# A two-layer transformer kernel on one core: dense products as single float32 matmuls, weights kept as loaded, activations turned by TensorE

## The chip, the core and the metric

The kernel runs on one NeuronCore of a Trainium2 chip. The core has five engines with queues of their own: TensorE (PE in the profile; its weight loads are listed apart as PEld), VectorE (DVE), ScalarE (ACT), GpSimd (POOL) and SyncE (SP, which here issues most DMAs). The metric is the device time of one execution in microseconds (us). Matmul operands lie in SBUF (128 partitions), results in PSUM banks of 512 float32 values per partition.

## The reference

Two identical layers over 2048 rows of 640 values, each a sliding-window attention block and a feed-forward block, in float32:

```
def _A_ref(x, wqkv, wo):                       # H = 32 heads of Dh = 20, window W = 256
    qkv = (x @ wqkv).reshape(B, S, 3, H, Dh)
    scores = einsum("bhqd,bhkd->bhqk", q, k) * Dh ** -0.5
    scores = where(0 <= q_pos - k_pos < W, scores, -1e9)
    o = einsum("bhqk,bhkd->bhqd", softmax(scores), v)
    return o.reshape(B, S, D) @ wo

def _B_ref(x, w1, b1, w2, b2):                 # F = 1536
    h = x @ w1 + b1
    return relu(h) ** 2 @ w2 + b2

for layer in range(2):                         # the same weights in both
    x = x + _A_ref(layernorm(x), wqkv, wo)
    x = x + _B_ref(layernorm(x), w1, b1, w2, b2)
```

## The kernel before

**Tiling.** The 2048 rows are cut into 8 groups of T = 256 rows; with two layers that makes 16 units (`NU`), worked on one after the other. A unit has five dense stages and eight quads of attention. A quad is four heads.

**Dense stages.** `stage_qk` forms q and k turned (weights stationary, 256 columns of rows move), `stage_v` forms v (rows stationary, 320 columns move), `stage_o` multiplies the attention's output by `wo`, `stage_f` does both feed-forward products. All go through `mm3` (L335). Every operand is held as two float16 halves, `hi` and the remainder `low`, and a product is three matmuls of halves: hi x hi, hi x low, low x hi. Scales (`YS`, `WS`, `OS`) keep the halves in float16's range.

**How halves are made.** Weights: loaded as float32 into memory that is used later (`w1raw`, `w2raw`, `krow`, `vts`), then `convert` (L270) writes hi on ScalarE and low on VectorE. Normalized rows: for most units `cross` (L444) casts hi on ScalarE, subtracts low on VectorE, and turns each half by a crossbar transpose that SP's queue issues (`dma_start_transpose`); `ln_cross` and `ln_early` use it ahead of `stage_qk`, `y_cross` ahead of `stage_f`. Units 0 and 1, and three turns of `stage_y`, use `split_t` (L383) instead: TensorE transposes 3 and 2 blocks of 128 columns into a PSUM tile, ScalarE copies hi out, VectorE subtracts. The attention's output is split in `load_o` (L1023, L1026), the feed-forward's hidden values in `stage_f` (L1123, L1126).

**Attention.** For each quad `max_quad` puts scores into the PSUM banks `bb6` and VectorE takes row maxima (L719, L722); `exp_quad` puts the shifted scores into the same banks and ScalarE takes exponentials (L827), which POOL (L856) and VectorE (L865) mask; `pv_quad` multiplies them by v on TensorE in float32 (L933). `banks()` waits until the readers of the last scores are done. Maxima run three quads ahead (`LEAD`) and come back as rows through a crossbar transpose and a DMA (`max_cross`).

**Order.** All five engines run the order in which the program is recorded, and the recorder plans it with costs of its own. `post` queues a job for VectorE, ScalarE or POOL with a cost in ns, `step(ns)` moves TensorE's planned clock `now`, `Want` holds back a piece until its operands or one of two PSUM tiles (`mm`) should be free. `together` lays a unit's dense stages between its quads in proportion to their planned costs (`QKC`, `VC`, `OC`, `FCST`, `LNC`), and takes more dense work where a quad would wait. `mm3` books 109 ns for a matmul of 256 columns and 136 for 320:

```
for a, b in ((0, 0), (0, 1), (1, 0)):
    nc.tensor.matmul(acc, lhs(a, c), rhs(b, c), start=(k == 0), stop=(k == 3 * nk - 1))
```

`spin` (L350) runs float32 matmuls of the 128x128 identity at the start, 14 and then 7.

Of the kernel before, what the change touches and what calls it, by code (L numbers as in the profile page):

```python
# [16 lines left out]
P = 128  # L17
# [17 lines left out]
YS = 2.0 ** 10  # L35
WS = 2.0 ** 8
QS = 2.0 ** 3
OS = 2.0 ** 6
# [7 lines left out]
def kernel(ctx: ExitStack, tc: tile.TileContext, x, wqkv, wo, w1, b1, w2, b2, out):  # L46
# [49 lines left out]
    def set_sums(i):  # L96
        nc.vector.memset(vts[i][0][:, :, DH:DH + 1], 1.0 / OS)
        nc.vector.memset(vts[i][1][:, H * (DH + 1):], 0.0)
# [158 lines left out]
    wq_s = sb.tile([P, 2, KC, 3 * D], F16, name="wq_s")  # L257
    wo_s = sb.tile([P, 2, KC, D], F16, name="wo_s")
    w1_s = sb.tile([P, 2, KC, F], F16, name="w1_s")
    w2_s = sb.tile([P, 2, FC, D], F16, name="w2_s")  # L260
# [4 lines left out]
    w1raw = w1_s.rearrange("p a k n -> p (a k n)").bitcast(F32)  # L265
    w2raw = w2_s.rearrange("p a k n -> p (a k n)").bitcast(F32)
    hraw = sb.tile([P, 2 * FC * T // 2], F32, name="stg", tag="hh", bufs=1)
    gate, gate0, gate2 = [Job("S", 0.0, None, [], 0.0, 0) for i in range(3)]

    def convert(st, hi, low, n, load, *deps, prio=2):  # L270

        a = post("A", 20 + 0.9 * n, lambda: nc.scalar.activation(hi, st, AF.Copy, scale=WS), load, *deps, prio=prio)
        return post("D", 30 + 1.04 * n, lambda: nc.vector.scalar_tensor_tensor(low, st, WS, hi, op0=ALU.mult,
                                                                               op1=ALU.subtract), a, prio=prio)
# [3 lines left out]
    def load_wq():  # L278
        at = 0
        for lo, n in [(j * D + c, min(2 * P, D - c)) for c in (0, 2 * P, 4 * P) for j in range(2)] + [  # L280
                (2 * D + c, min(2 * P, D - c)) for c in (0, 2 * P, 4 * P)]:
            raw, o = (w1raw, at) if at + KC * n <= FC * D else (krow[2], at - FC * D)
            at += KC * n
            st = raw[:, o:o + KC * n].rearrange("p (c n) -> p c n", c=KC)
            load = dma(lambda st=st, lo=lo, n=n:
                       nc.sync.dma_start(st, wqkv[:, lo:lo + n].rearrange("(c p) n -> p c n", p=P)),
                       P * KC * n * 4, prio=0, land=WLAND)
            for z in range(0, n, P):
                c = slice(lo + z, lo + z + P)
                wqj[(lo + z) // P] = convert(st[:, :, z:z + P], wq_s[:, 0, :, c], wq_s[:, 1, :, c], KC * P, load,  # L290
                                             prio=1)
# [3 lines left out]
    def load_wo():  # L295

        v = wo.rearrange("(p c) n -> p c n", c=KC)
        raw = w2raw[:, (FC - KC) * D:].rearrange("p (c n) -> p c n", n=D)
        loads = []
        for c0, n in ((0, 2), (2, 3)):  # L300
            loads.append(bulk(lambda c0=c0, n=n: nc.scalar.dma_start(raw[:, c0:c0 + n], v[:, c0:c0 + n]), P * n * D * 4, gate0))
        for c in range(KC):
            woj[c] = convert(raw[:, c], wo_s[:, 0, c], wo_s[:, 1, c], D, loads[-1], *loads[:-1])
        rowset[1] = [post("D", 460, lambda k=k: set_row(1, k), prio=2) for k in range(4)]

    def load_w1():
        first = list(wqj.values())
        for f0 in (0, 6, 2, 8, 4, 10):
            st = w2raw[:, f0 * D:(f0 + 2) * D].rearrange("p (c n) -> p c n", c=KC)
            load = bulk(lambda st=st, f0=f0: nc.scalar.dma_start(  # L310
                st, w1[:, f0 * P:(f0 + 2) * P].rearrange("(c p) n -> p c n", p=P)), P * KC * 2 * P * 4, gate,
                *(woj.values() if (f0 + 2) * D > (FC - KC) * D else ()))
            for f in (f0, f0 + 1):
                c = slice(f * P, (f + 1) * P)
                w1j[f] = convert(st[:, :, (f - f0) * P:(f - f0 + 1) * P], w1_s[:, 0, :, c], w1_s[:, 1, :, c], KC * P,
                                 load, *first)

    sums = []

    def load_w2():  # L320
        used_by = {}
        for c, place in enumerate((3, 4, 0, 1, 2, 0, 1, 2, 0, 1, 2, 0)):
            first = [w1j[f] for f in (c // 4 * 2, c // 4 * 2 + 1, 6 + c // 4 * 2, 7 + c // 4 * 2)]
            st = vts[1 + place][1][:, :D] if place > 2 else krow[2][:, D * place:D * (place + 1)]
            load = bulk(lambda st=st, c=c: nc.scalar.dma_start(st, w2[c * P:(c + 1) * P, :]), P * D * 4,
                        *([w2j[used_by[place]]] if place in used_by else [gate] if place > 2 else [gate, gate2]))
            w2j[c] = convert(st, w2_s[:, 0, c], w2_s[:, 1, c], D, load, *first)
            used_by[place] = c
        sums.extend(post("D", 130, lambda i=i: set_sums(4 + i), w2j[used_by[3 + i]], prio=2) for i in range(2))


# [3 lines left out]
    def mm3(acc, lhs, rhs, nk, ns, then=None):  # L335

        k, t = 0, 0.0
        for c in range(nk):
            for a, b in ((0, 0), (0, 1), (1, 0)):
                nc.tensor.matmul(acc, lhs(a, c), rhs(b, c), start=(k == 0), stop=(k == 3 * nk - 1))  # L340
                k += 1
                t += ns
                if t >= STEP and k < 3 * nk:
                    yield t
                    t = 0.0
# [13 lines left out]
    def layernorm(src, y, *deps, prio=2):  # L359
# [8 lines left out]
        def var():  # L368
            box["mv"] = mv = sb.tile([P, 4], F32, name="bmv", bufs=2)
            nc.vector.bn_aggr(mv[:, 0:2], box["st"])  # L370
            nc.vector.tensor_scalar(mv[:, 2:3], mv[:, 1:2], 1e-5, YS ** -2, op0=ALU.add, op1=ALU.mult)
# [11 lines left out]
    def split_t(y, dst, job, made, bb=None):  # L383
# [5 lines left out]
        def out(tr, jobs, c0, n, wait):  # L389
            j = post("A", 170 * n, lambda: nc.scalar.copy(dst[:, 0, c0:c0 + n], tr[:, :n]), wait=wait, prio=0)  # L390
            j = post("D", 170 * n, lambda: nc.vector.tensor_sub(dst[:, 1, c0:c0 + n], tr[:, :n], dst[:, 0, c0:c0 + n]), j,  # L391
                     prio=0)
# [42 lines left out]
    def ln_t(u, yT=None):  # L435
        ys = lns.pop(u)
        if yT is None:
            yT = sb.tile([P, 2, KC, T], F16, name="yT", tag="yT", bufs=1)
        yTs[u], pre[u] = yT, []
        bb = banks() if u == 0 else (None, None)  # L440
        for i in range(2):
            yield from split_t(ys[i][0], yT[:, :, :, i * P:(i + 1) * P], ys[i][1], pre[u], bb[i])

    def cross(ys, dst, room, prio=2):  # L444

        box = {}
        js, out, j = [], [], None
        for i, (y, ready) in enumerate(ys):
            def high(i=i, y=y):
                if i == 0:  # L450
                    box["yl"] = room()
                    box["dst"] = dst()
                nc.scalar.copy(box["yl"][:, i, 0], y)

            def low(i=i, y=y):
                yl = box["yl"]
                nc.vector.tensor_sub(yl[:, i, 1], y, yl[:, i, 0])

            def turn(a, i=i):
                nc.sync.dma_start_transpose(box["dst"][:, a, :, i * P:(i + 1) * P], box["yl"][:, i, a])  # L460

            j = post("A", 615, high, ready, j, prio=prio)
            out.append(dma(lambda turn=turn: turn(0), P * D * 2, j, cost=1250.0, land=CROSS))
# [964 lines left out]
```

## Time and profile before

| | |
|---|---|
| time, median of 2 runs | 1557.72 us (1557.5 to 1557.95) |
| the profiled execution | 1555.59 us |
| its span in the trace | 1553.9 us |
| mean granted TensorE clock | 0.998 |
| PE busy | 1530.8 us, 25832 matmul records |
| VectorE busy | 1036.8 us |
| ScalarE busy | 670.0 us |
| GpSimd busy | 453.0 us |
| DMA | 162.34 MB, 104 GB/s over the span |

A group row names line, engine, operation, output and inputs, shape and count, then busy time in us and the mean ns of one instruction, then the idle time before them and what ended it. In the timeline a row gives start, length, engine, line and count; neighbours of one kind are merged, and the length runs to the last one's end. In a table of windows the columns are the stretch, its length, busy time and count of PE, PEld, DVE, ACT and POOL, the granted clock, DMA share and GB/s. Durations of matmuls are latencies in a pipeline: the distance from start to start is what a matmul takes of the engine.

### The profile page before, as it was taken

To read this page: it belongs to the slowest core of one execution; us is meant where nothing else is said; L and a number is where in the kernel's file an instruction comes from. 1 tells how busy PE (TensorE), PEld (TensorE's weight loads), DVE (VectorE), ACT (ScalarE), POOL (GpSimd) and SP (SyncE) were. 2 spreads that over 40 slices of the span, in tenths; PEclk is the share of its full clock that TensorE was granted. 3 is DMA by queue.
4 is the path that set the end of the run, shared out by engine and by line. 5 is a ranking of instruction groups with operands and counts; after the bars stand their busy time and mean duration, and the time that the engine had idled before them with its cause. 6 is when DMAs were issued, how large, how long until landed. Compare 5 with 4: busy or idle time off the path is not lost.

```text
span 1553.9 us, 58533 instructions
## 1 busy us (share of the span) xinstructions
PE 1530.8 (99%) x25832; PEld 1197.5 (77%) x25832; DVE 1036.8 (67%) x2246; ACT 670.0 (43%) x1367; POOL 453.0 (29%) x847
## 2 busy tenths in 40 slices
PE   8998999999999999999999999999999999999999
PEld 7766778787787877778777787877878777786777
DVE  8788775666766567665656767667665676767641
ACT  4564445344443534534343443444435345354422
POOL 1223314133231322314132241332314224142321
PEclk9999999999999999999999999999999999999999
DMA  9773353442534334343353434435343352432010
GB/s 283 206 224 100 78 130 86 117 101 80 127 69 125 86 105 114 61 128 79 110 130 65 122 82 130 89 81 128 67 131 79 104 121 62 121 86 64 27 62 18
DMA packets 240343, 162.34 MB, mean 104 GB/s; under 512 B 93016, under 2 KB 224088, under 8 KB 240088
## 3 DMA queue, kind: packets, MB, share of 16 engines
q1 hardware_dynamic: 234136, 149.09, 38.0%
q10 hardware_dynamic: 5952, 9.50, 2.1%
q8 instruction: 203, 3.33, 0.9%
q14 instruction: 52, 0.43, 0.1%
HBM read 79.76 MB, written 58.72 MB: 89 GB/s over the span
## 4 chain that ended last, share of the span: by engine, by line
PE 94%; DVE 3%; ACT 1%; issue 1%; POOL 0%; ACTq 0%; DVEq 0%; POOLq 0%
PE acc L340 74%; PE pv L933 8%; PE bb L705 5%; PE bb L842 5%; PE bb L933 2%; ACT pt L827 1%; DVE mx L722 1%; DVE bb L685 0%; PE bb L737 0%; PE bb L888 0%; DVE bb L719 0%; DVE qd L538 0%; POOL pt L856 0%; PE tr L404 0%; DVE mx L685 0%
## 5 line engine op out<-in xcount | busy, mean ns | idle before, releaser
L827 ACT ACTIVATE pt<-bb 128x640 f32<-128x640 f32 (+2 forms) x512 | 312.5, 683 | 164.7 <-PE bb L842 141.0
L856 POOL TENSOR_SCALAR_AFFINE_SELECT pt<-pt 64x256 f32<-64x256 f32 x448 | 198.5, 443 | 595.9 <-ACT pt L827 566.7
L340 PE MATMUL acc<-y,w_s 128*128 128x256 f16 x2880 | 330.3, 273 | 2.3 <-DVE y L391 2.1
L340 PE MATMUL acc<-w_s,hh 128*128 128x320 f16 (+1 forms) x2340 | 326.7, 297 | 0.1
L340 PEld LDWEIGHTS <-w_s 128*128 128x128 f16 x2880 | 276.2, 98 | 42.1 <-issue 3.2
L340 PEld LDWEIGHTS <-hh 128*128 128x128 f16 x2340 | 222.1, 98 | 86.8 <-issue 0.4
L722 DVE TENSOR_REDUCE mx<-bb 128x4 f32<-128x1024 f32 x224 | 273.1, 1223 | 6.7
L340 PE MATMUL acc<-yT,wq_s 128*128 128x256 f16 x2250 | 259.0, 273 | 2.4 <-DVE mT L797 0.7
L340 PEld LDWEIGHTS <-wq_s 128*128 128x128 f16 x2400 | 229.6, 98 | 36.5 <-issue 3.4
L865 DVE COPY_PREDICATED_SCALAR pt<-drop,zero 128x256 f32 x224 | 99.8, 498 | 138.9 <-ACT pt L827 138.6
L1121 POOL TENSOR_TENSOR r<-r 128x256 f32<-128x256 f32 x192 | 122.6, 659 | 214.6 <-ACT r L1117 212.0
L945 ACT COPY ot<-pv 128x256 f32<-128x256 f32 x128 | 47.7, 372 | 287.5 <-PE bb L933 255.3
L933 PE MATMUL pv<-pt,vt 64*32 64x128 f32 (+5 forms) x3840 | 168.1, 303 | 0.9 <-ACT vt L624 0.9
L1127 DVE TENSOR_TENSOR hh<-r,hh 128x256 f16<-128x256 f32 x192 | 90.5, 484 | 108.7 <-ACT hh L1124 104.3
L933 PE MATMUL bb<-pt,vt 64*32 64x192 f32 (+3 forms) x3584 | 154.6, 302 | 0.4 <-POOL pt L856 0.4
L719 DVE COPY_PREDICATED bb<-maskq,bb 128x256 f32<-128x256 uint16 x224 | 94.0, 424 | 84.8 <-PE bb L705 84.1
L933 PEld LDWEIGHTS pv<-pt,vt 64*32 64x32 f32 (+1 forms) x3840 | 126.1, 106 | 31.5 <-issue 3.3
L340 PE MATMUL acc<-wo_s,od 128*128 128x320 f16 x960 | 139.6, 300 | 2.1 <-ACT od L1024 2.0
L340 PE MATMUL acc<-wq_s,yT 128*128 128x320 f16 x900 | 130.4, 299 | 1.6 <-DVE kt L391 0.5
L1117 ACT ACTIVATE r<-acc,b1s 128x256 f32<-128x256 f32 x192 | 81.2, 477 | 95.3 <-PE acc L340 93.4
L340 PEld LDWEIGHTS <-od 128*128 128x128 f16 x960 | 91.1, 98 | 40.4 <-ACT od L1024 2.3
L933 PEld LDWEIGHTS bb<-pt,vt 64*32 64x32 f32 x3584 | 116.3, 106 | 1.6 <-POOL pt L856 0.9
(105 smaller groups left out, 1444.8 us busy)
## 6 DMA issues: line engine op xcount, KB each, us to landing
o<-ot SPq DMA_DIRECT2D x64, 256.0 KB
qt<-qk SPq DMA_DIRECT2D x30, 480.0 KB
kt<-qk SPq DMA_DIRECT2D x30, 480.0 KB
qk<-qd SPq DMA_DIRECT2D x15, 640.0 KB
od<-o SPq DMA_DIRECT2D x14, 640.0 KB
qk<-yl SPq DMA_DIRECT2D x13, 640.0 KB
xt<-in_A_x_dram SPq DMA_DIRECT2D x16, 320.0 KB
x<-in_A_x_dram SPq DMA_DIRECT2D x16, 320.0 KB
```

What stands on the lines that cost most here:

```text
L340: nc.tensor.matmul(acc, lhs(a, c), rhs(b, c), start=(k == 0), stop=(k == 3 * nk - 1))
L705: nc.tensor.matmul(flat[e][rows, o:o + b - a], qt[r, p, i * P + 64 * h:i * P + 64 * (h + 1)], kt[r, p, a + to:b + to], start=True, stop=Tr ...
L719: nc.vector.copy_predicated(wins[:, :, 4 * Q:], later, wins[:, :, :Q])
L722: nc.vector.tensor_reduce(most, wins[:, :, Q:], axis=mybir.AxisListType.X, op=ALU.max)
L827: return lambda: nc.scalar.activation(room_of(box)[:, a:b], bank[:, a:b], AF.Exp, scale=SCALE / (QS * QS))
L842: nc.tensor.matmul(flat[e][h * Q:(h + 1) * Q, c0:c1], kt[r, 2 * qd + j, k0:k0 + Q], qt[r, 2 * qd + j, q:q + c1 - c0], start=True, stop=Tru ...
L856: nc.gpsimd.affine_select(out=m, in_=m, pattern=[[0, 4], [-1 if k else 1, Q]], base=0, fill=0.0, compare_op=ALU.is_gt if k else ALU.is_ge, ...
L865: nc.vector.copy_predicated(m, drop[:, k:k + 1, :].bitcast(mybir.dt.uint16).to_broadcast([P, 4, Q]), zero.unsqueeze(1).to_broadcast([P, 4, ...
L933: nc.tensor.matmul(pv[h][32 * jj:32 * (jj + 1), q0 * Q:(q0 + w) * Q], vf[r, c:c + 32], boxes[e]["pt"][r, a:b], start=(k == 0), stop=(k == ...
L1117: nc.scalar.activation(box["r"], acc[:, f, :], AF.Relu, bias=b1s[:, f0 + f:f0 + f + 1], scale=1.0 / (YS * WS))
L1121: nc.gpsimd.tensor_tensor(box["r"], box["r"], box["r"], op=ALU.mult)
L1127: nc.vector.tensor_sub(hh[:, 1, f, :], box["r"], hh[:, 0, f, :])
```

## The change

Operands are kept in float32 and a product is one float32 matmul instead of three of halves. The weights are loaded straight to their places; `convert` and the staging are gone, and with them the scales. `w1` comes without waiting for `wq`'s conversion, `w2` in six DMAs instead of twelve. `cross`, `ln_early`, `ln_cross` and `y_cross` are gone: all 16 units' normalized rows are turned through `split_t`, which has one copy on ScalarE in place of the copy and the subtraction, before `stage_qk` (`ln_t`) and before `stage_f` (`stage_y`). `load_o` ends with the division, `stage_f` with the square. The planner books 218 and 272 ns for a product, and its sums of costs are lowered to match.

```diff
-    def mm3(acc, lhs, rhs, nk, ns, then=None):
+    def product(acc, lhs, rhs, nk, ns, then=None):
-        k, t = 0, 0.0
+        t = 0.0
         for c in range(nk):
-            for a, b in ((0, 0), (0, 1), (1, 0)):
-                nc.tensor.matmul(acc, lhs(a, c), rhs(b, c), start=(k == 0), stop=(k == 3 * nk - 1))
-                k += 1
-                t += ns
-                if t >= STEP and k < 3 * nk:
+            nc.tensor.matmul(acc, lhs(c), rhs(c), start=(c == 0), stop=(c == nk - 1))
+            t += ns
+            if t >= STEP and c < nk - 1:
...
-    wq_s = sb.tile([P, 2, KC, 3 * D], F16, name="wq_s")
+    wq_s = sb.tile([P, KC, 3 * D], F32, name="wq_s")
...
-            load = dma(lambda st=st, lo=lo, n=n:
-                       nc.sync.dma_start(st, wqkv[:, lo:lo + n].rearrange("(c p) n -> p c n", p=P)),
-                       P * KC * n * 4, prio=0, land=WLAND)
+            load = dma(lambda lo=lo, n=n: nc.sync.dma_start(
+                wq_s[:, :, lo:lo + n], wqkv[:, lo:lo + n].rearrange("(c p) n -> p c n", p=P)),
+                P * KC * n * 4, prio=0, land=WLAND)
...
         def out(tr, jobs, c0, n, wait):
-            j = post("A", 170 * n, lambda: nc.scalar.copy(dst[:, 0, c0:c0 + n], tr[:, :n]), wait=wait, prio=0)
-            j = post("D", 170 * n, lambda: nc.vector.tensor_sub(dst[:, 1, c0:c0 + n], tr[:, :n], dst[:, 0, c0:c0 + n]), j,
-                     prio=0)
+            j = post("A", 170 * n, lambda: nc.scalar.copy(dst[:, c0:c0 + n], tr[:, :n]), wait=wait, prio=0)
...
-                yield from mm3(acc[:, c, :], lambda a, k: wq_s[:, a, k, lo:lo + P],
-                               lambda b, k: yT[:, b, k, :], KC, 109, evict if c == n - 1 else None)
+                yield from product(acc[:, c, :], lambda k: wq_s[:, k, lo:lo + P],
+                                   lambda k: yT[:, k, :], KC, 218, evict if c == n - 1 else None)
...
-            def high(q=q):
-                nc.scalar.copy(od[:, :, 0, q], val[:, :, q])
-
-            def low(q=q):
-                nc.vector.tensor_sub(od[:, :, 1, q], val[:, :, q], od[:, :, 0, q])
...
-                    def square(box=box):
-                        nc.gpsimd.tensor_tensor(box["r"], box["r"], box["r"], op=ALU.mult)
-
-                    def high(box=box, f=f0 + f):
-                        nc.scalar.copy(hh[:, 0, f, :], box["r"])
-
-                    def low(box=box, f=f0 + f):
-                        nc.vector.tensor_sub(hh[:, 1, f, :], box["r"], hh[:, 0, f, :])
+                    def square(box=box, f=f0 + f):
+                        nc.gpsimd.tensor_tensor(hh[:, f, :], box["r"], box["r"], op=ALU.mult)
...
-    QKC, VC, OC, FCST, LNC, CARRY, KEEP, MID = 16.4e3, 8.2e3, 8.2e3, 39.2e3, 1.2e3, 18e3, 24e3, 10e3
+    QKC, VC, OC, FCST, LNC, CARRY, KEEP, MID = 10.9e3, 5.5e3, 5.5e3, 26.2e3, 1.2e3, 14e3, 18e3, 7e3
...
-            parts += [stage_qk(u + 1, (0,)), stage_v(u + 1, range(2)), stage_o(u - 1), lambda: (y_cross(u - 1), iter(()))[1], stage_qk(u + 1, (1,)), stage_v(u + 1, range(2, 4))]
-            cost += QKC + VC
+            parts += [ln_t(u + 1), stage_qk(u + 1, (0,)), stage_v(u + 1, range(2)), stage_o(u - 1), stage_qk(u + 1, (1,)), stage_v(u + 1, range(2, 4)), stage_y(u - 1)]
+            cost += QKC + VC + 2 * LNC
```

The order of instructions moves with the costs. On TensorE, between the exp scores of a unit's last quad and the scores for the maxima that follow them. Before, a block of the next unit's q stands between (50 matmuls of `yT` and `wq_s`; the first is shown). `bb` are the score banks, `kt` and `qt` the turned k and q:

```order
L842 LDWEIGHTS kt_97
L842 MATMUL bb_143<-qt,kt_97 64x64
L842 LDWEIGHTS kt_97
L842 MATMUL bb_144<-qt,kt_97 64x64
L340 LDWEIGHTS wq_s
L340 MATMUL acc<-yT,wq_s 128x256
```

After, at the same place, line 757 is what was line 842 and line 620 what was line 705:

```order
L757 LDWEIGHTS kt_97
L757 MATMUL bb_143<-qt,kt_97 64x64
L757 LDWEIGHTS kt_97
L757 MATMUL bb_144<-qt,kt_97 64x64
L620 LDWEIGHTS qt
L620 MATMUL bb_143<-kt_95,qt 64x256
```

The dense block is gone from between them: the last quad's exp scores and the next scores for maxima stand side by side. In the whole order this is so at 16 places, at a 17th the p x v itself follows its exp scores, and at 21 places exp scores follow a p x v directly. Before there is none of these; one place has only two transposes between. The dense work of a unit now stands in its first seven quads.

On ScalarE, over the same part of a unit. Before (`pt` exponentials, `r` the relu, `hh` its halves, `ot` the p x v result, `yl` the halves of rows for the crossbar):

```order
L1117 ACTIVATE r<-acc,b1s 128x256 x2
L827 ACTIVATE pt<-bb_143 128x640
L827 ACTIVATE pt<-bb_144 128x640
L827 ACTIVATE pt<-bb_143 128x640
L827 ACTIVATE pt<-bb_144 128x640
L1124 CAST hh<-r 128x256
L1117 ACTIVATE r<-acc,b1s 128x256 x2
L1124 CAST hh<-r 128x256 x3
L945 COPY ot<-pv 128x256
```

After, where `yT` is the copy of TensorE's transposes for the unit after:

```order
L742 ACTIVATE pt<-bb_143 128x640 x2
L742 ACTIVATE pt<-bb_144 128x640 x2
L860 COPY ot<-pv 128x256
L742 ACTIVATE pt<-bb_143 128x640
L742 ACTIVATE pt<-bb_144 128x640
L742 ACTIVATE pt<-bb_143 128x640
L742 ACTIVATE pt<-bb_144 128x640
L860 COPY ot<-pv 128x256
L355 COPY yT<-tr 128x3x128
L355 COPY yT<-tr 128x2x128
```

The casts to halves have left the queue, the last quads' exponentials follow each other with one copy between, and the copies of the turn have come in.

On TensorE at a turn, after the last p x v of a unit (there is no such place before in these units: the rows were turned by SP's queue, where 54 crossbar transposes of `yl` stood that are gone now):

```order
L848 MATMUL pv<-pt,vt_102 32x64
L848 MATMUL bb_144<-pt,vt_99 32x64
L367 MATMUL tr<-ident,xt 128x128 x10
L306 MATMUL acc<-yT,wq_s 128x256 x13
L757 LDWEIGHTS kt_96
```

Ten transposes, in four groups of 3, 2, 3 and 2 through the two PSUM tiles, stand right ahead of the product that reads them. There are 320 such transposes now, 50 before; the other 270 make 27 turns.

More of the change, by code (lines that the diff above doesn't have):

```diff
@@ L318 @@
-    sums = []
-    def load_w2():
[L321 to L329, printed above, removed]
+            c = slice(f0 * P, (f0 + 2) * P)
```

171 lines of the change are left out of this document (52 added, 119 removed).

## The prediction

> **What bounds the kernel now.** I read the page's shares first, then the groups by shape, then stretches of the timeline. The first rows say which engine sets the time.
>
> ```profile
> span 1553.9 us, 58533 instructions
> ...
> PE 1530.8 (99%) x25832; PEld 1197.5 (77%) x25832; DVE 1036.8 (67%) x2246; ACT 670.0 (43%) x1367; POOL 453.0 (29%) x847
> ...
> PE 94%; DVE 3%; ACT 1%; issue 1%; POOL 0%; ACTq 0%; DVEq 0%; POOLq 0%
> ```
>
> TensorE is busy for all but 23 us, and 94% of the chain is its own. So whatever adds TensorE time adds to the end, and work taken off VectorE (67%) or ScalarE (43%) is worth nothing by itself. Nearly all of TensorE is the dense products of line 340. By shape:
>
> ```profile
> L340 PE MATMUL acc<-y,w_s 128*128 128x256 f16 x2880 | 330.3, 273 | 2.3 <-DVE y L391 2.1
> L340 PE MATMUL acc<-w_s,hh 128*128 128x320 f16 x2268 | 321.7, 299 | 0.1
> L340 PE MATMUL acc<-yT,wq_s 128*128 128x256 f16 x2250 | 259.0, 273 | 2.4 <-DVE mT L797 0.7 <-DVE qd L538 0.6 <-DVE wq_s L273 0.6
> L340 PE MATMUL acc<-wo_s,od 128*128 128x320 f16 x960 | 139.6, 300 | 2.1 <-ACT od L1024 2.0
> L340 PE MATMUL acc<-wq_s,yT 128*128 128x320 f16 x900 | 130.4, 299 | 1.6 <-DVE kt L391 0.5 <-DVE mT L797 0.3 <-DVE yl L538 0.3
> ...
> L340 PE MATMUL acc<-kt,wq_s 128*128 128x256 f16 x150 | 17.5, 273 | 0.0
> ...
> L340 PE MATMUL acc<-wq_s,kt 128*128 128x320 f16 x60 | 9.1, 299 | 0.0
> ...
> L340 PE MATMUL acc<-w_s,hh 128*128 128x160 f16 x72 | 5.1, 233 | 0.0
> ```
>
> 5280 matmuls of 256 columns, 4188 of 320, 72 of 160. The mean of one (273 ns) is its latency, not its price, as they are pipelined; the price is the distance from start to start, read from unbroken runs:
>
> ```profile
> 702.41 4.00 PE L340 MATMUL acc<-yT,wq_s 128*128 128x256 f16 x35
> ...
> 1497.21 8.31 PE L340 MATMUL acc<-wo_s,od 128*128 128x320 f16 x60
> ...
> 8.72 1.73 PE L354 MATMUL spin<-ident 128*128 128x128 f32 x14
> ...
> 1507.54 0.71 PE L404 MATMUL bb<-ident,xt 128*128 128x128 f32 x5
> ```
>
> Taking one latency off each run: (4.00 - 0.27)/34 = 109.6 ns for 256 float16 columns and (8.31 - 0.30)/59 = 135.8 ns for 320, so 0.41 ns a column and about 4 ns fixed. The dense work is 5280 x 0.1096 + 4188 x 0.1358 + 72 x 0.070 = 1152 us, 74% of the span.
>
> **What one float32 product costs.** The kernel has float32 matmuls already, and two things show in them. First, each stands twice in the trace: the third row above is the second warm-up (7 matmuls in the program) with 14 records, and both warm-ups (14 + 7) have 42:
>
> ```profile
> L354 PEld LDWEIGHTS spin<-ident x42: 190/192/338, 1.4 to 10.1; 128*128 128x128 f32 x42
> L354 PE MATMUL spin<-ident x42: 274/275/579, 1.4 to 10.2; 128*128 128x128 f32 x42
> ```
>
> Second, a record streams slower. At 128 columns it takes (1.73 - 0.275)/13 = 112 ns, 0.87 ns a column. The p x v products, float32 on 64x32 pieces of the array, show the same at other widths (first row of each pass or chunk):
>
> ```profile
> 701.11 0.40 PE L933 MATMUL pv<-pt,vt 64*32 64x256 f32 x1
> ...
> 701.35 0.38 PE L933 MATMUL pv<-pt,vt 64*32 64x256 f32 x1
> ...
> 701.56 0.27 PE L933 MATMUL pv<-pt,vt 64*32 64x128 f32 x1
> ...
> 701.78 0.32 PE L933 MATMUL pv<-pt,vt 64*32 64x192 f32 x1
> ```
>
> 256 columns: two records in 0.45 us; 128 columns: two in 0.22 us. That is 0.225 and 0.110 us a record, 0.90 ns a column, twice float16's. So one float32 product is two records at double the time each, four float16 passes' worth, where the kernel now issues three. The code's planner books 218 ns for 256 columns, which is one such record, not both.
>
> Dense after: 3180 products, 6360 records: 3520 of 256 columns, 2792 of 320, 48 of 160. A record of 256 lies between 216 ns (twice the streaming of float16, fixed part once) and 224 ns (twice the warm-up's 112); 320 between 269 and 280. I take 218 and 271.5, nearer the lower ends since a fixed part need not double: 767 + 758 + 7 = 1532 us, **+380** (from +367 to +423).
>
> The Trainium skill, "FP8 and Floating Point Precision" (TensorE Precision Notes), says that true float32 takes four passes through the array. At the 2.4 GHz of "TensorE: Matmul & The Clock Gate" that would be, as an estimate, 901,120 columns x 4 / 2.4 = 1502 us, +350, with a total of 2086 us; it speaks against this change, and the records' distances above bear it out.
>
> **What is removed.** The casts and subtractions that make halves leave VectorE and ScalarE, for instance
>
> ```profile
> L1127 DVE TENSOR_TENSOR hh<-r,hh 128x256 f16<-128x256 f32 x192 | 90.5, 484 | 108.7 <-ACT hh L1124 104.3
> ```
>
> and with them the weights' conversions, and 54 crossbar transposes on SP's queue. All of it ran beside a busy TensorE, so it gives nothing; the queues behind it only get shorter. The longer turns put 108 copies of some 0.43 us (rows below) on ScalarE instead, 46 us on an engine at 43%: nothing but the wait priced below. Loads of weights keep their bytes and go straight to their places: nothing.
>
> **What moves to TensorE.** 27 more unit-turns of 10 float32 transposes. A transpose has one record; (0.71 - 0.273)/4 = 109 ns: 270 x 0.109 = **+29**. Each turn goes through two PSUM tiles and ScalarE copies, and the product behind it needs the last copy:
>
> ```profile
> 1508.28 0.48 ACT L390 CAST y<-bb 128x384 f16<-128x384 f32 x1 [8.50 <-PE bb L404]
> ...
> 1509.59 0.37 ACT L390 CAST y<-bb 128x256 f16<-128x256 f32 x1 [0.82 <-DVE y L391]
> ```
>
> Four copies of 0.48, 0.37, 0.48, 0.37 = 1.7 us, plus about 0.7 us of hand-overs, less the 1.1 us of transposes: 1.3 us of standing still a turn. At least 0.5 (the last copy and its hand-over), at most 1.9 if none overlaps: 27 x 1.3 = **+35** (14 to 51).
>
> **What the new order uncovers.** The planner paces attention as if dense work took half of what it will, and pulls it forward. The order of TensorE then has, at the end of nearly every unit, quads with nothing between: 17 places where the next attention step follows the exp scores directly, 21 where exp scores follow a p x v directly. Both write the same PSUM banks, so TensorE must wait for ScalarE, or for VectorE. The kernel before has one such spot:
>
> ```profile
> 128.57 0.92 PE L842 MATMUL bb<-qt,kt 62*64 62x128 f16 x38
> 129.41 0.44 PE L404 MATMUL tr<-ident,xt 128*128 128x128 f32 x2
> 132.11 0.27 PE L705 MATMUL bb<-kt,qt 60*64 60x256 f16 x1 [2.26 <-ACT pt L827]
> 132.71 0.75 PE L705 MATMUL bb<-kt,qt 60*64 60x256 f16 x37 [0.33 <-ACT pt L827]
> ```
>
> The lengths that have to be covered, from a quiet stretch:
>
> ```profile
> 691.10 0.42 DVE L719 COPY_PREDICATED bb<-maskq,bb 128x256 f32<-128x256 uint16 x1
> 691.55 1.23 DVE L722 TENSOR_REDUCE mx<-bb 128x4 f32<-128x1024 f32 x1
> ...
> 695.40 0.76 PE L842 MATMUL bb<-qt,kt 62*64 62x128 f16 x38
> ...
> 696.34 2.49 ACT L827 ACTIVATE pt<-bb 128x640 f32<-128x640 f32 x4 [5.14 <-PE bb L842]
> ```
>
> Exponentials end 698.83 - 696.16 = 2.67 us after their scores: 2.8 with a hand-over. The maxima need 2 x (0.42 + 1.23) = 3.3 us, of which the p x v (1.3 us) covers some: 1.9 remain. 17 x 2.8 + 21 x 1.9 = 88, and about 10 where only 4 products or a small transpose stand between: 98, less some 6 that the span has already: **+92**. Half of it if the queues run ahead in the long dense stretches (50), half more if other VectorE and ScalarE work stands first (140).
>
> **The clock.** Beside that spot stands a drop:
>
> ```profile
> 128.00:131.00 3.00, 1.85 (x46) 1.38 (x44) 2.74 (x6) 1.59 (x4) 0.00 (x0) 1.00 0.00 0
> 131.00:134.00 3.00, 1.56 (x55) 1.11 (x61) 2.96 (x9) 1.66 (x3) 1.74 (x3) 1.00 0.32 93
> 134.00:137.00 3.00, 1.34 (x63) 0.80 (x47) 2.05 (x4) 0.37 (x1) 2.85 (x5) 1.00 0.47 134
> 137.00:141.00 4.00, 3.04 (x16) 2.15 (x17) 3.88 (x7) 2.02 (x4) 2.23 (x3) 0.64 0.25 79
> ```
>
> After 9 us with TensorE busy for 4.75 the mean clock of 4 us falls to 0.64: 3.4 us lost half their speed, if dense work fills them 1.7 us of work. The end of each of 14 units will be as sparse: 14 x 1.7 = **+24** (0 if dense work sets in before, 50 with two drops each).
>
> In the Trainium skill, "TensorE: Matmul & The Clock Gate" (Part 1), the clock halves after an idle window of about 3.4 us. Here the longest gap was 2.26 us and it fell all the same, so the row decides; read strictly, the rule charges no drops, and the sum would be 2092 us.
>
> **Sum.** Against the profiled execution: 1553.9 + 380 + 29 + 35 + 92 + 24 = 2114 us of span; 1.7 us lie around it (1555.59 beside 1553.9), so 2116 us. The median of the runs is 1557.72, 2 us above the profiled one; a difference of 2% of it (31 us) is about what a measurement tells from no change.
>
> **Rivals.**
> - *One column a cycle after all, faster.* If the warm-up's 112 ns is not streaming but its 128-column weight load, a record of 256 columns could cost 112 ns and one of 320 138 ns, the planner's 218 for a product. Dense 394 + 385 + 5 = 784 us, -368; transposes, turns, waits and drops as above, with some 45 more of waits, an estimate, since cover is half as long: 1553.9 - 368 + 225 = 1411, about 1413 us. It decides below 132 ns a record of 256 columns, where the dense work saves just the 225 us that the rest costs. Against it: p x v, whose loads have 32 columns, scales with its columns at 0.90 ns. 4%.
> - *Weight loads come into the open, far slower.* A float32 load lasts 192 ns in the rows above; if all that exceeds a cover of about 98 ns, 94 ns, showed per record: 6360 x 0.094 = 598 more, 2714 us. Against: the warm-up's loads of 192 ns come every 112 ns, so they overlap. 2%. The Trainium skill, "TensorE: Matmul & The Clock Gate" (Weight-path perf modes), excludes float32 from fast weight loading, which would lengthen the load; no run here shows what that does behind 256 columns.
> - *The waits vanish.* Slow dense work lets the other engines run ahead, no bare quad costs anything: 1553.9 + 380 + 29 + 14 = 1977, 1979 us. Against: exponentials can't start before their scores. 8%.
> - *The order hurts everywhere.* VectorE and ScalarE queues, ordered for dense groups half as long, hold a maximum or exponential behind an eviction, 1 us in each of 128 quads: 2116 + 128 = 2244 us. For it: both queues hold evictions between these. Against: where they do, dense work follows on TensorE. 8%.
> - *My forecast*: 78%.
>
> **Numbers.** The likeliest is 2116 us. All low ends give 1553.9 + 367 + 29 + 14 + 50 + 2 = 2016, all high ends 2249, which together are unlikely; with part of the two slower-side rivals I take 2000 to 2210. Faster by over 2% is the first rival, 0.04; within 2% needs a dense record between the two prices, 0.01; slower 0.95.
>
> **What would show it.** Right: 6360 dense records, starts 216 to 224 ns apart at 256 columns; a dense sum near 1530 us; TensorE waiting for exponentials (some 45 us) and for maxima (some 40) once per unit, for ScalarE copies after turns; many drops of the clock; VectorE well below 1036.8 us without being waited for more than that. Wrong: 3180 records, or 256 columns every 112 ns, or TensorE's idle time still near 23 us.

## The result and the profile after

The changed kernel takes 2174.78 us (median of 2 runs, 2173.89 to 2175.68) against 1557.72 before: a ratio of 1.3961, 95% interval 1.3901 to 1.4021. The span of its profiled execution is 2172.2 us, 618.3 more than before. The forecast was 2116, the range 2000 to 2210.

First the page's shares, and TensorE's rows over 40 slices of the span, after the change:

```profile
PE 2040.5 (94%) x22922; PEld 1542.4 (71%) x22922; DVE 847.1 (39%) x1872; ACT 561.5 (26%) x1121; POOL 420.3 (19%) x847
...
PE   9979999999999999999899999999999999997969
...
PEclk9978999999999999999999999999999999998989
```

TensorE has 2910 records fewer and is busy 510 us longer. VectorE lost 190 us and ScalarE 109, and it bought nothing. TensorE's share fell from 99% to 94%: 132 us now pass in which it does nothing, 23 before. (The page's chain of waits broke off after 3% of this span and isn't used.)

The dense groups by shape (line 306 is the new product; count, then busy us and mean ns of one, then idle time before):

```profile
L306 PE MATMUL acc<-y,w_s 128*128 128x256 f32 x1920 | 435.4, 385 | 2.9 <-ACT y L355 1.3 <-issue 0.5
L306 PE MATMUL acc<-w_s,hh 128*128 128x320 f32 x1512 | 429.4, 437 | 0.0
L306 PE MATMUL acc<-yT,wq_s 128*128 128x256 f32 x1500 | 338.2, 382 | 4.5 <-ACT yT L355 3.7 <-DVE qd L453 0.8
```

Two thirds of the old counts (2880, 2268, 2250), not one third: each float32 product is two records. Two unbroken rows of the timeline (start, length, count) give the price:

```profile
711.05 5.55 PE L306 MATMUL acc<-wq_s,yT 128*128 128x320 f32 x20
...
733.32 13.22 PE L306 MATMUL acc<-y,w_s 128*128 128x256 f32 x60
```

(13.22 - 0.38)/59 = 218 ns at 256 columns and (5.55 - 0.43)/19 = 269 ns at 320. The same division of the rows before gave 109.6 and 135.8.

TensorE's longest lists of waits after the change (us in total, times, longest):

```profile
PE bb L620 <- ACT pt L742: 40.5, 44, 2.1
PE bb L757 <- DVE mx L637: 34.8, 30, 2.2
PE acc L306 <- DVE ov L932: 11.1, 2, 9.8
```

The score banks wait for exponentials and for maxima, 75 us in all. The 9.8 us of the third row are one wait near the end of the span, ahead of a product with `wo`. One end of a unit with such waits in TensorE's timeline (line 620 scores for maxima, 757 scores for exponentials, 367 transposes; square brackets hold the idle time before and its releaser):

```profile
649.82 0.76 PE L620 MATMUL bb<-kt,qt 60*64 60x256 f16 x38
...
652.84 0.21 PE L757 MATMUL bb<-qt,kt 62*64 62x128 f16 x1 [0.26 <-DVE mx L637]
654.84 1.28 PE L757 MATMUL bb<-qt,kt 62*64 62x128 f16 x37 [1.78 <-DVE mx L637]
658.25 0.37 PE L620 MATMUL bb<-kt,qt 60*64 60x256 f16 x1 [2.13 <-ACT pt L742]
658.85 1.28 PE L620 MATMUL bb<-kt,qt 60*64 60x256 f16 x37 [0.23 <-ACT pt L742]
662.37 2.73 PE L367 MATMUL tr<-ident,xt 128*128 128x128 f32 x10
665.31 5.88 PE L306 MATMUL acc<-yT,wq_s 128*128 128x256 f32 x26 [0.21 <-ACT yT L355]
```

Two things show: gaps of 1.78 and 2.13 us, and 38 score matmuls that took 0.76 us at 649.82 but 1.28 us for 37 at 654.84 and 658.85. The windows over the same place give the reason in their third last column, the granted clock:

```profile
652.00:655.00 3.00, 0.95 (x45) 0.78 (x37) 2.87 (x5) 0.37 (x1) 0.00 (x0) 0.94 0.05 18
655.00:658.40 3.40, 1.26 (x38) 1.07 (x34) 0.18 (x1) 2.09 (x4) 0.08 (x1) 0.50 0.04 10
658.40:662.00 3.60, 3.37 (x90) 2.31 (x95) 2.54 (x4) 0.40 (x1) 1.58 (x4) 0.50 0.03 7
662.00:666.00 4.00, 3.65 (x37) 2.58 (x22) 1.98 (x3) 1.93 (x5) 0.00 (x0) 0.64 0.10 37
```

From 654.66 to 664.90 TensorE ran at half speed (the trace's record of the clock gives the two ends). In that record there are 23 such stretches, mostly of 6.8 or 10.2 us, 178 us in all; before there were 3, 8 us.

To close the sum, each TensorE record is charged with the distance from its start to the next record's start, so that waits and slow clock fall on the work ahead of them and the parts add up to the time from the first matmul to the last, 4 to 5 us less than the span. The table has all kernels of this document; "idle" and "half clock" are contained in the other columns, and warm-up and filling matmuls are left out.

| kernel | time | ratio (95%) | span | dense | transposes | attention | idle | half clock |
|---|---|---|---|---|---|---|---|---|
| before | 1557.72 | | 1553.9 | 1186.8 | 13.2 | 341.7 | 18.7 | 8.1 |
| after | 2174.78 | 1.396 (1.390-1.402) | 2172.2 | 1589.3 | 73.9 | 496.9 | 127.2 | 178.1 |
| e1_costs | 1982.05 | 1.273 (1.268-1.278) | 1980.3 | 1570.6 | 67.8 | 329.1 | 16.8 | 2.0 |
| e2_four | 1927.53 | 1.238 (1.233-1.243) | 1925.6 | 1565.8 | 13.2 | 334.1 | 11.1 | 12.7 |
| e4_fill | 2144.44 | 1.377 (1.371-1.384) | 2145.5 | 1590.6 | 68.9 | 396.5 | 61.4 | 41.0 |
| e5_noturn | 2166.85 | 1.392 (1.386-1.397) | 2164.8 | 1617.2 | 0 | 535.4 | 154.3 | 226.2 |
| e7_book | 1855.84 | 1.193 (1.190-1.196) | 1851.3 | 1269.3 | 13.7 | 556.1 | 211.3 | 213.3 |
| e8_two | 1488.29 | 0.956 (0.954-0.958) | 1489.2 | 954.5 | 17.7 | 504.7 | 228.2 | 227.1 |
| e9_early | 1994.79 | 1.283 (1.280-1.285) | 1993.0 | 1570.6 | 79.8 | 330.0 | 27.9 | 3.1 |
| e10_twobooked | 1410.92 | 0.906 (0.903-0.908) | 1412.5 | 873.9 | 14.5 | 511.2 | 192.9 | 31.6 |

(Idle here is the time in which no matmul record runs, between the first and the last.) So the 618 us are +402.5 dense, +60.7 transposes and +155.2 attention, although attention's instructions did not change.

### The profile page after: what moved, and what is told of

Read it like the earlier page. It is cut to its first block, busy times and chain, and to the rows that moved or that the text cites. A ratio compares the mean times of both kernels' runs of the same rounds, so it can differ in the third digit from the quotient of the medians.

```text
span 2172.2 us, 51928 instructions
## 1 busy us (share of the span) xinstructions
PE 2040.5 (94%) x22922; PEld 1542.4 (71%) x22922; DVE 847.1 (39%) x1872; ACT 561.5 (26%) x1121; POOL 420.3 (19%) x847
## 5 line engine op out<-in xcount | busy, mean ns | idle before, releaser
L306 PE MATMUL acc<-y,w_s 128*128 128x256 f32 x1920 | 435.4, 385 | 2.9 <-ACT y L355 1.3
L306 PE MATMUL acc<-w_s,hh 128*128 128x320 f32 (+1 forms) x1560 | 435.9, 433 | 0.0
L306 PEld LDWEIGHTS acc<-y,w_s 128*128 128x128 f32 x1920 | 362.3, 191 | 59.0 <-ACT y L355 6.2
L306 PEld LDWEIGHTS acc<-w_s,hh 128*128 128x128 f32 x1560 | 287.7, 190 | 113.5 <-issue 0.6
L306 PE MATMUL acc<-yT,wq_s 128*128 128x256 f32 x1500 | 338.2, 382 | 4.5 <-ACT yT L355 3.7
L306 PEld LDWEIGHTS acc<-yT,wq_s 128*128 128x128 f32 x1500 | 281.2, 190 | 49.0 <-ACT yT L355 6.7
L306 PE MATMUL acc<-wo_s,ov 128*128 128x320 f32 x640 | 189.3, 452 | 12.7 <-DVE ov L932 11.1
L306 PE MATMUL acc<-wq_s,yT 128*128 128x320 f32 x600 | 171.9, 437 | 0.1
L306 PEld LDWEIGHTS acc<-wo_s,ov 128*128 128x128 f32 x640 | 122.3, 197 | 67.7 <-issue 18.2
L1015 POOL TENSOR_TENSOR hh<-r 128x256 f32<-128x256 f32 x192 | 113.8, 614 | 268.0 <-ACT r L1011 266.8
L620 PE MATMUL bb<-kt,qt 60*64 60x64 f16 (+3 forms) x4256 | 103.5, 235 | 40.5 <-ACT pt L742 40.5
```

Source lines behind the costliest of these rows:

```text
L306: nc.tensor.matmul(acc, lhs(c), rhs(c), start=(c == 0), stop=(c == nk - 1))
L620: nc.tensor.matmul(flat[e][rows, o:o + b - a], qt[r, p, i * P + 64 * h:i * P + 64 * (h + 1)], kt[r, p, a + to:b + to], start=True, stop=Tr ...
L1015: nc.gpsimd.tensor_tensor(hh[:, f, :], box["r"], box["r"], op=ALU.mult)
```

## The experiments

### e1_costs: the planner's costs put right

The changed kernel, with the price of a product as two records and the sums of costs doubled to match. Nothing that is computed changes, only the order.

```diff
-                                   lambda k: yT[:, k, :], KC, 218, evict if c == n - 1 else None)
+                                   lambda k: yT[:, k, :], KC, 432, evict if c == n - 1 else None)
...
-                                   lambda k: wo_s[:, k, hs], KC, 272,
+                                   lambda k: wo_s[:, k, hs], KC, 540,
...
-    QKC, VC, OC, FCST, LNC, CARRY, KEEP, MID = 10.9e3, 5.5e3, 5.5e3, 26.2e3, 1.2e3, 14e3, 18e3, 7e3
+    QKC, VC, OC, FCST, LNC, CARRY, KEEP, MID = 21.6e3, 10.8e3, 10.8e3, 51.8e3, 1.2e3, 24e3, 32e3, 13e3
```

> The changed kernel with only the planner's bookings altered: 432 and 540 ns for a product instead of 218 and 272, and the sums of costs doubled, so that every quad has dense work around it again. The arithmetic is the same. Theory A (of the 618 us lost, some 370 are float32's passes, some 60 the turns, and the rest waits and clock drops that come of an order planned for half the dense time): TensorE's waits for exponentials and maxima fall from 84 us to under 15, half-clock time from 178 us to under 30, and the time from 2175 to 2000 to 2040 us. Rival B (the waits don't matter, since the slow dense work is the bound everywhere): 2150 us or more. Rival C (the dense order hurts VectorE's and ScalarE's queues in general): waits move elsewhere, time between 2050 and 2150.

Measured: 1982.05 us, 193 less than after, and lower than I had allowed for. TensorE's longest waits of this kernel:

```profile
PE acc L306 <- ACT yT L355: 6.3, 13, 0.5
PE tr L367 <- ACT yT L355: 4.6, 13, 0.4
PE tr L367 <- ACT vt L539: 2.4, 12, 0.2
```

The waits for exponentials are gone and those for maxima are down to 0.5 us; half-speed time fell from 178 to 2 us, attention is back at 329 us. So about 192 us of the 618 (2172.2 - 1980.3) came from the order that the wrong prices and sums made, and 426 from the work itself: +384 dense, +55 transposes, -13 attention.

### e2_four: four float16 passes in the old order

The kernel before with the fourth product of halves (low x low) behind every low x hi; order, halves and turns stay.

```diff
-                nc.tensor.matmul(acc, lhs(a, c), rhs(b, c), start=(k == 0), stop=(k == 3 * nk - 1))
+                nc.tensor.matmul(acc, lhs(a, c), rhs(b, c), start=(k == 0), stop=False)
+                if a:
+                    nc.tensor.matmul(acc, lhs(1, c), rhs(1, c), start=False, stop=(k == 3 * nk - 1))
```

> The kernel before with a fourth matmul of halves, low x low, in every product (12720 float16 matmuls in place of 9540), its plan and order kept. If a float32 product costs what four float16 matmuls cost and the dense work is TensorE's bound, this is the changed kernel's dense price in the old order: 3180 more matmuls, 1760 at 109.6 ns, 1396 at 135.8, 24 at 70 = 384 us, so 1940 us (1925 to 1955). If a fourth pass could hide behind something (TensorE not the bound), under 1900. If the longer dense work brings clock drops or waits of itself, over 1980.

Measured: 1927.53 us, 371 more than the 1556.8 of the same session. Its dense sum is 1565.8 us, that of e1_costs, which does the same products in float32, 1570.6. One float32 product costs what four float16 products cost. The rest of e1_costs over this kernel, 54.7 us of span, is as much as the transposes add (67.8 - 13.2 = 54.6); dense work has 5 us more there and attention 5 us less.

### e4_fill: bare quads filled with dense matmuls of the identity

The changed kernel, its order kept; 309 more float32 matmuls of the 128x128 identity into the warm-up's PSUM tile, 7 ahead of exponentials' scores and 9 ahead of maxima's scores, only where attention follows attention without dense work between, which makes a quad bare (`apart` is the planner's mark of that).

```diff
+    def fill(k):
+        if apart[0]:
+            spin(k)
...
+        fill(9)
...
+        fill(7)
```

> The changed kernel with matmuls of the identity put on TensorE where an attention step follows another without dense work between: 9 ahead of scores for maxima, 7 ahead of exp scores (309 in all, some 69 us of TensorE inside its 131 us of idle time). They keep the engine busy and change nothing else. Theory A (the clock drops come from sparse stretches and cost about 60 us, mostly by attention's own matmuls at half speed): half-clock time from 178 us to under 70, the waits stay, time from 2175 to 2105 to 2140 us. Rival B (halves fall into waits and cost nothing): the clock recovers but the time stays within 15 us of 2175. Rival C (the fillers themselves stand in the way): slower.

Measured: 2144.44 us, 30 less, just short of the expected gain, though TensorE does 77 us more of work that nobody needs. The waits that it stands in for shrank:

```profile
PE bb L621 <- ACT pt L748: 7.4, 27, 1.3
PE bb L763 <- DVE mx L638: 5.8, 15, 1.1
```

Half-speed time went from 178 to 41 us, and idle time from 127 to 61. Idle time that turns into filler gives nothing, and the filler took 11 us more than the idle time that went; so the gain must come from attention running at full speed. In the table attention loses 100 us; 68 of it is idle time that went from behind attention's records (106 to 38 us), and 32 us are shorter records. Some 6 of these are not clock: in a gap the last matmul counts with its whole latency, some 0.23 us, and with a filler behind it only with its distance, which is about 0.17 less at each of 38 bare places. By this comparison the slow clock costs the changed kernel's attention some 26 us.

### e5_noturn: transposes left out

ScalarE copies the rows as they are; the ten transposes of each turn are left out.

```diff
-            j = post("A", 170 * n, lambda: nc.scalar.copy(dst[:, c0:c0 + n], tr[:, :n]), wait=wait, prio=0)
+            j = post("A", 170 * n, lambda: nc.scalar.copy(dst[:, c0:c0 + n], y[:, c0 * P:(c0 + n) * P].rearrange("p (c n) -> p c n", n=P)), wait=wait, prio=0)
...
-            for c in range(n):
-                nc.tensor.transpose(tr[:, c, :], y[:, (c0 + c) * P:(c0 + c + 1) * P], ident)
```

> The changed kernel without the 320 transposes on TensorE: ScalarE copies the rows as they are, in the same number of copies and the same order, so what is left out is the turning itself. Theory A (a turn costs TensorE its transposes and a wait for copies, 27 x 2.4 us by the prediction, 61 us by start distances in the two traces): time from 2175 to 2105 to 2125 us. Rival B (the turns fill waits that would be there anyway): 2150 us or more.

Measured: 2166.85 us, only 8 less than after, in spite of 320 records fewer, and in the rival's range. Waits of this kernel, and one turn in its timeline:

```profile
PE acc L306 <- ACT yT L355: 20.7, 13, 1.7
PE acc L306 <- ACT y L355: 20.3, 15, 4.7
```

```profile
660.19 1.53 ACT L355 COPY yT<-xt 128x384 f32<-128x384 f32 x4
...
661.47 8.82 PE L306 MATMUL acc<-yT,wq_s 128*128 128x256 f32 x26 [1.67 <-ACT yT L355]
```

The four copies run after the work of the unit ahead, and the product waits 1.67 us for them, with or without transposes. In the sums, the transposes' 74 us went, and idle time at other places came in, 39 us more (115 to 154), nearly all between attention and dense work, where the copies are waited for. What is left, 35 us, is what 320 transposes at 109 ns take of the engine. Of these, 28 were lost again: half-speed time grew by 48 us, and the dense column by 28. So the wait for the copies is a cost of its own beside the transposes, and in the changed order the clock takes back most of what shorter work gives.

### e9_early: turns moved ahead of need

On top of e1_costs: the turn of the next unit between the halves of the feed-forward's second product, and the turn for the feed-forward ahead of v.

```diff
+            if i and ahead is not None:
+                yield from ln_t(ahead)
...
-            parts += [ln_t(u + 1), stage_qk(u + 1, (0,)), stage_v(u + 1, range(2)), stage_o(u - 1), stage_qk(u + 1, (1,)), stage_v(u + 1, range(2, 4)), stage_y(u - 1)]
+            parts += [stage_qk(u + 1, (0,)), stage_v(u + 1, range(2)), stage_o(u - 1), stage_qk(u + 1, (1,)), stage_y(u - 1), stage_v(u + 1, range(2, 4))]
```

> The kernel of the first experiment (float32 products, bookings right) with the turns moved away from the products that read them: the next unit's rows are turned between the two halves of the second feed-forward product, the others ahead of the v product. Theory A (a turn costs its transposes, some 36 us in all, and about 20 us of TensorE waiting for ScalarE's copies): the waits go, the transposes stay, time from 1982 to 1960 to 1970 us. Rival B (transposes are hidden and the copies' wait is all of it): TensorE's start distances of transposes fall under 20 us, time under 1950. Rival C (waits for copies were only the place where other waits showed): 1975 or more.

Measured: 1994.79 us, 13 more than e1_costs; the gain that I expected did not come, and the time lies where the last rival had it. The waits:

```profile
PE tr L367 <- DVE kd L453: 7.9, 13, 0.6
PE acc L306 <- ACT y L355: 6.9, 13, 0.5
PE acc L306 <- ACT yT L355: 6.4, 12, 0.5
```

The product behind a turn does not read the turned rows here, and still waits for the turn's copy; the transposes wait for an eviction of k (`kd`). Transposes and products share the two PSUM tiles `mm`, so whatever follows a turn needs a tile that a copy has to free. That the tiles are the reason is read from the program and from who waits; no run had a third tile. Moving the reader away changes who waits, not that someone waits.

### e7_book: the old kernel with prices too low

The kernel before, every float16 product still done three times, but booked at two thirds (72 and 90 ns) with the lowered sums of the changed kernel. It shows what the lower prices do without any change of the work. (One small edit more lets the recorder go on where the dense pieces of the first units run out; e8_two has it too.)

```diff
-                               lambda b, k: yT[:, b, k, :], KC, 109, evict if c == n - 1 else None)
+                               lambda b, k: yT[:, b, k, :], KC, 72, evict if c == n - 1 else None)
...
-                               lambda c, k: wo_s[:, c, k, hs], KC, 136,
+                               lambda c, k: wo_s[:, c, k, hs], KC, 90,
...
-    QKC, VC, OC, FCST, LNC, CARRY, KEEP, MID = 16.4e3, 8.2e3, 8.2e3, 39.2e3, 1.2e3, 18e3, 24e3, 10e3
+    QKC, VC, OC, FCST, LNC, CARRY, KEEP, MID = 10.9e3, 5.5e3, 5.5e3, 26.2e3, 1.2e3, 14e3, 18e3, 7e3
```

> The kernel before, arithmetic and crossbar turns kept, with the planner's bookings lowered to two thirds: 72 and 90 ns for a float16 matmul instead of 109 and 136, so that a product books 216 and 270 ns and the sums of costs are those of the changed kernel. Theory A (the changed kernel's waits come from the bookings and not from float32): attention steps stand bare at the ends of units here too, waits for exponentials and maxima rise from under 10 us to 60 to 110, some clock drops, and the time goes from 1557 to 1640 to 1740 us. Rival B (the waits come of float32 and the turns): within 30 us of 1557.

Measured: 1855.84 us, 300 more than before for the same instructions, more than any theory had. Its waits:

```profile
PE bb L705 <- ACT pt L827: 92.1, 75, 9.0
PE bb L842 <- DVE mx L722: 42.3, 29, 2.5
PE bb L842 <- DVE ot L948: 12.3, 6, 3.3
```

The same pair of waits as in the changed kernel, at the same places of the program, with 213 us at half speed. The mechanism is shown a second time, on work that did not change. That it costs more here than in the changed kernel (300 against 192) fits ScalarE's casts, which still stand in its queue between exponentials (676 us busy against 562); that step was not tried by itself.

### e8_two and e10_twobooked: two passes, planned in two ways

Both are the kernel before with hi x hi and hi x low alone. e8_two tells the planner what this costs: 109 and 136 ns a matmul, and the sums (`QKC` to `MID`) of the changed kernel. e10_twobooked leaves the planner with the prices of three passes, 163.5 and 204 ns for each matmul that is left and the sums of before, so that the order stays that of before. The edit that they share, and then that of e10_twobooked's price:

```diff
-            for a, b in ((0, 0), (0, 1), (1, 0)):
+            for a, b in ((0, 0), (0, 1)):
...
-                               lambda b, k: yT[:, b, k, :], KC, 109, evict if c == n - 1 else None)
+                               lambda b, k: yT[:, b, k, :], KC, 163.5, evict if c == n - 1 else None)
```

> The kernel before with two matmuls of halves in every product, hi x hi and hi x low; the third, low x hi, is left out, so the products lose one operand's remainder. The planner's sums are lowered to match. If the number of passes through TensorE sets the time: 3180 fewer matmuls, 384 us less, 1173 us, plus waits since attention has less dense work to stand behind: 1190 to 1260 us. If VectorE (busy for 1037 us before, as many casts) becomes the bound: 1260 to 1400.

> The kernel before with two passes (hi x hi and hi x low; low x hi is left out, so weights count in full and rows only to float16), but the planner keeps the numbers of three: 163.5 and 204 ns a matmul, the sums as before. So the order is that of before with every third dense matmul taken out of its place, where the two passes run before were planned with the true, lower costs and came to 1488 us with 228 us of idle TensorE. Theory A (what costs time when dense work is booked below or at its price is the order: dense work drawn to the front of a unit, bare quads at its end): with dense work left between all quads, TensorE's idle time falls below 120 us, the clock's half-speed time below 80 us, and the time is 1250 to 1340 us (1557 - 384 of streaming, plus waits where cover is a third thinner). Theory B (with a third less cover the other engines bound the quads, whatever the order): idle time stays near 200 us, the time within 40 us of 1488.

Measured: 1488.29 and 1410.92 us. The first is slower than either range expected of it, the second lies between the ranges of its two theories. A third of the dense records less is 384 us of streaming; e8_two kept 67 of it, e10_twobooked 145. Waits of e8_two:

```profile
PE bb L705 <- ACT pt L827: 40.9, 38, 2.6
PE bb L842 <- DMA qt<-mt: 33.0, 26, 2.8
PE acc L340 <- ACT od L1024: 30.0, 13, 10.0
```

Waits of e10_twobooked, and its chain of waits by engine:

```profile
PE bb L842 <- DVE ot L948: 48.8, 52, 1.5
PE bb L842 <- DVE mx L722: 21.6, 16, 2.1
...
PE bb L705 <- ACT pt L827: 5.6, 9, 1.0
```

```profile
DVE 40%; PE 25%; ACT 10%; DMA 8%; POOL 7%; issue 7%; SPq 2%; ACTq 0%; DVEq 0%; POOLq 0%
```

Each theory of the second run was right on one point and wrong on the time. Half-speed time fell from 227 to 32 us in the two profiled executions, as the first had it, and the time by 77. But idle time only fell from 228 to 193 us, as the second had it: VectorE is on 40% of the chain, where TensorE was on 94% before. That a third less dense work to stand behind is the reason fits this and was not tried by itself. Nor is the clock shown to be what the 77 us are made of: another execution of e10_twobooked had a mean clock of 0.94, where the profiled one had 0.989, and its span, 1410.1 us, lies among the others' 1403.8 to 1412.5. So in this kernel the order alone does not fix the clock, and a slower clock did not show in the time. e10_twobooked ran faster than both kernels, at the price of the products of low halves of rows.

## Why the prediction was right, step by step

The forecast of 2116 was 59 us too low, and the mechanism it named was the one found. Some small slips in its working change nothing: the p x v rows give 0.88 and 0.86 ns a column where it says 0.90, its rule for the low end of 320 columns gives 267.6 ns and not 269, and 3.3 less 1.3 us leave 2.0 for the maxima and not 1.9.

- **Dense work, +380.** Right. Records start 218 and 269 ns apart where 218 and 271.5 were taken, and there are two to a product. With the costs put right the dense sum grew by 384 us, and four float16 passes in the old order, by 379. The Trainium skill's four passes of true float32 ("FP8 and Floating Point Precision", TensorE Precision Notes) agree with e2_four: 1565.8 us of dense work beside the 1570.6 of e1_costs. The first two rivals (a column a cycle; exposed weight loads) are out by the same rows.
- **Turns, +29 and +35.** Right in sum: 64 forecast, +60.7 measured, +54.6 in e1_costs. The reason was half right. The wait at a turn was put down to the product that reads the turned rows; e9_early shows it at products that don't read them; what these share with the turn is the two PSUM tiles.
- **Waits that the order uncovers, +92.** Right. At the 38 bare places TensorE stood idle for 83 us where 88 were taken (44 where exp scores follow a p x v, 37 where scores for maxima follow exp scores, 2.6 where a p x v follows its own exp scores). The lists of waits have 40.5 us for exponentials where 17 x 2.8 = 48 were taken, and 34.8 for maxima where 21 x 1.9 = 40 were. All idle time behind attention's records grew by 100 us (from 7 to 106); 9.8 of it are the single wait near the end, which no term had, so that 100 stands so close to 92 is in part luck. e1_costs takes them away by order alone, e7_book makes them by order alone. So the rival in which they vanish fell. Of the one in which every quad of a unit suffers nothing shows: the waits stand where quads are bare.
- **The clock, +24.** Too small; this is the mis-sized term. The step that failed was the length of a drop: 3.4 us for each of 14 units, from the one drop that the old trace shows beside a bare spot (3.41 us in its record of the clock; the row shown has 2.9 of them inside its window). Measured are 6.8 or 10.2 us for most units, and twice 17 to 34. It was also assumed that the dense work behind the bare quads pays; instead the attention of the bare quads itself runs at half speed, as the 1.28 us in the timeline shows. What it cost can be counted in the trace: each TensorE record that starts at half speed and has no gap behind it is set against the mean distance of its like at full speed (same line and shape, same neighbours). That makes about 59 us, 41 in attention, 13 in dense work and 5 in transposes. It is an estimate, as records ahead of a gap are left out. The same count for e4_fill gives 13 us. Of the difference its time shows 30, and its fillers took 11 more than the idle time that went; 5 stay open.
- **Work taken off VectorE and ScalarE: nothing.** Right. 190 and 109 us fewer on these engines, while the time grew by what TensorE got.

The sum over the terms was 2114 of span for 2172.2: of the 58 us missing, attention has 39 (155 for 92 + 24), dense work 22, and turns gave back 3. Of attention's 155, 100 are idle time and about 41 the clock. The 14 that are left fit matmuls that count with their whole latency ahead of a gap, for which the prediction had no term; no run parts these from the rest.

## What to carry to other kernels

Before one replaces several float16 passes by one float32 pass, count records, not instructions: here a float32 matmul is two records of double length, worth four float16 passes, so three passes of halves were the cheaper way. Where an order is planned from prices, measure each price as the distance from start to start in an unbroken run and enter it before judging the change; prices at half of their true value, with the sums that go with them, cost 192 us here, and at two thirds of it 300 us in the old kernel. And a planner with true prices is not the end either: after a third of the dense work was gone, the order planned with the dearer prices was the better one by 77 us.

## What the runs showed of the hardware

The clock fell with TensorE partly busy. These are the windows of the spot shown, cut where the record of the clock has its steps:

```profile
651.24:654.66 3.42, 1.55 (x61) 1.31 (x60) 3.29 (x5) 0.37 (x1) 0.00 (x0) 1.00 0.26 101
654.66:658.07 3.41, 1.28 (x37) 1.10 (x37) 0.48 (x3) 1.76 (x3) 0.00 (x0) 0.50 0.04 10
658.07:661.48 3.41, 3.00 (x78) 2.12 (x85) 2.16 (x4) 0.73 (x2) 1.66 (x4) 0.50 0.03 7
661.48:664.90 3.42, 3.28 (x50) 2.26 (x34) 2.37 (x4) 1.29 (x4) 0.00 (x0) 0.50 0.00 0
```

In the 3.42 us ahead of the fall TensorE was busy for 1.55, and no gap that began there was longer than 1.78 us. Two stretches later it was busy for 3.00 us of 3.41, and the clock stayed at half for one more. All steps of the clock inside this span are whole multiples of 3.41 us apart. Its 22 falls came behind stretches of that length in which TensorE was busy for 17 to 51%. Of the stretches at full clock that no fall followed, the lowest was busy for 46%, the next for 54%. Full speed came back behind stretches of 84 to 100%, and half speed stayed behind stretches of up to 88%. So what goes with a fall here is the busy share of the stretch ahead of it, with the turning point near a half.

Total idle time does not tell how much clock is lost: in the profiled executions e10_twobooked stood still for 193 us and was at half speed for 32, while the changed kernel stood still for 127 and was slow for 178. What differed was how the idle time was spread: 38 stretches of the changed kernel were busy for less than half, and 8 of e10_twobooked. Ten more of e10_twobooked lay between 50 and 56%, and no fall followed them. That its other execution had 0.94 of the clock may come of such stretches falling under the limit; no trace of it shows that.

The Trainium skill, "TensorE: Matmul & The Clock Gate" (Part 1), has the clock halve after an idle window of about 3.4 us. The lengths of the drops here, all but a last one that the end cuts off, are multiples of 3.41 us, which fits a window of that length, but the engine was not idle through one, so on the condition the trace differs.
